# Moving an attention kernel's output projection into the gaps of late units, and its last piece into half of the last V's place

## The chip, the core and the metric

The kernel runs on one core of one Trainium2 chip. The metric is the device time of one execution in microseconds (us), as a median of several runs.

The engines of the core are named as in the profile: PE (matrix engine), DVE (vector engine), ACT (scalar engine), POOL (idle here), and SP, whose queue issues all data transfers. Each load of K, V and the weights is carried by 16 DMA engines. In lines of the profile, PEld is the weight load of PE, SPq is SP's queue, and L580 is line 580 of that kernel's file; a line number can shift by one or more between kernels.

## The reference, cut

Two layers, each a single-token decode step of attention over a long cache, followed by a small MLP block:

```python
def _A_ref(x, k_cache, v_cache, wq, wo):          # x: 2x1x576, caches: 2x32x16384x128 bf16
    q = (x @ wq) split in 32 heads of 128
    p = softmax(q . k * 128 ** -0.5)
    return (p . v, heads side by side) @ wo        # wo: 4096x576
x = x + _A_ref(_layernorm(x), ...);  x = x + _B_ref(_layernorm(x), ...)   # and once more, the same weights
```

K and V of the 2 x 32 heads are 512 MB together and are read twice, once per layer, but for two units that layer 1 still finds in place. All the rest is small.

## The kernel before

A *unit* is one head of one batch entry: 4 MB of K and 4 MB of V. A layer has 64 units. For each, half of the scores is made on PE (transposes of K chunks, then products) and half on DVE (a multiply and a sum per chunk of 1024 columns); PE weighs V one unit later.

K and V come into three *places* of 8 MB, each with a K half and a V half. The list of loads is worked off in order: a load is issued when everything that lies under its target has been used.

```python
        def kv(kind, l, i, split=False):
            ...                                   # place pl: K half at pl*place_n, V half at +unit; the last K and V in two parts
        ...
            for i in range(U):
                kv("K", l, i, split=(l == 1 and i == 2) or i == U - 1)
                ...
                    kv("V", l, i - 1)
                j, r = divmod(i - wo_at, gap)
                if r == 0 and 0 <= j < self.n_wo:
                    want_wo(l, j, wp * self.place_n + (unit if j == self.n_wo - 1 else j * self.WO_PIECE * D))
                if l == 0 and i == 6:
                    want_w2(wp * self.place_n + 5 * unit // 4)
            for i in range(U - 3, U):
                kv("V", l, i, split=i == U - 1)
            want_w34(l, 1, 1 if l == 0 else 2)     # weights of the MLP, then wq of the next layer
```

The output projection by `wo` is cut in eight pieces: seven of four heads, and one of three heads (`N_MID`). They are loaded early, into the place that the layer's last unit (63) will use: seven pieces in its K half, the last piece and `w2` in its V half. So the last K waits for the seven pieces, and the last V waits for the last piece:

```python
    def attention(self, l):
        ...
            if i == last + 1:                      # unit 57
                if l == 0:
                    self.shift_term()              # uses w2
                self.project_pieces(l, range(self.n_wo - 1))
            ...
                if i == U - 1 and c == 5:          # unit 63, after chunk 5 of 8
                    self.weigh(l, i - 2, 0)
                    self.weigh(l, i - 2, 1)
                    self.project_pieces(l, [self.n_wo - 1])
```

`project_pieces` makes the softmax normalizers on PE and DVE, scales the outputs on DVE, and runs five small matmuls per head on PE. PE's program is a hardware loop over two units at a time for units 2 to 55 of layer 0 and 12 to 55 of layer 1; its other units are straight code.

```python
        with self.nc.Block() as block:
            for e in self.ENGS:
                def run(eng, items=plan[e], loops=self.loops if e == "tensor" else ()):
```

## Time and profile before

The median was 2588.58 us in three runs. From the page of the kernel before: the busy time of each engine, the mean busy share of the 16 DMA engines in 40 slices, the bytes per second in the same slices, and the data queue with its share of 16 engines' span.

```profile
PE 1549.2 (60%) x34519; PEld 1463.6 (57%) x34519; DVE 1977.2 (76%) x2775; ACT 1112.9 (43%) x1809; POOL 0.8 (0%) x10
...
DMA  9999999999999999999899999999999999999997
GB/s 412 431 429 431 430 431 430 431 433 431 431 430 430 431 431 433 430 428 409 371 420 428 429 425 434 431 429 431 432 432 429 430 434 431 431 430 433 418 427 324
...
q1 hardware_dynamic: 51944, 1097.76, 99.1%
```

The memory stream bounds the kernel: 431 GB/s nearly everywhere, and DVE, the next, 76% busy. The dips are at the end of layer 0 (371) and at the end (324). Closer, in windows of 5 us of the kernel before (the columns are the busy time of PE, PEld, DVE, ACT and POOL with the number of instructions, the granted PE clock, the mean busy share of the DMA engines, and GB/s):

```profile
1160.00:1165.00 5.00, 3.83 (x147) 3.77 (x144) 4.90 (x7) 1.61 (x3) 0.00 (x0) 0.59 0.92 390
1165.00:1170.00 5.00, 2.20 (x20) 1.93 (x20) 4.68 (x9) 2.21 (x3) 0.00 (x0) 0.50 0.61 208
...
1265.00:1270.00 5.00, 4.96 (x148) 4.86 (x145) 4.93 (x6) 2.45 (x6) 0.00 (x0) 0.50 0.47 200
1270.00:1275.00 5.00, 1.07 (x22) 1.08 (x23) 4.21 (x10) 0.00 (x0) 0.00 (x0) 0.50 0.04 16
1275.00:1280.00 5.00, 5.00 (x160) 5.00 (x158) 3.33 (x4) 2.05 (x2) 0.00 (x0) 0.50 0.92 318
```

These are two holes: a small one at 1165 and a large one at 1270. Layer 1 has the same two near 2435 and 2540. Their causes stand in the timelines. First PE, with the start, the time, what it did, and in brackets the idle time before and what ended it:

```profile
1145.63 3.89 PE L580 MATMUL misc<-otn,buf 128*128 128x2 bf16 x140 [1.16 <-DVE otn L765]
...
1184.72 1.89 PE L670 MATMUL tps<-ident,buf 128*128 128x128 bf16 x16 [1.21 <-DMA buf<-in_A_k_cache_dram]
...
1242.98 1.89 PE L670 MATMUL tps<-ident,buf 128*128 128x128 bf16 x16 [4.58 <-DMA buf<-in_A_k_cache_dram]
```

The burst of 140 matmuls is the projection of seven pieces before unit 57; the others are the first work on K of unit 59 and of unit 62, both of which PE waited for. Then SP's queue, which shows when transfers were issued:

```profile
1141.83 0.33 SPq L359 DMA_DIRECT2D buf<-in_A_k_cache_dram  x1
...
1168.04 0.33 SPq L359 DMA_DIRECT2D buf<-in_A_k_cache_dram  x1
...
1221.82 16.81 SPq L359 DMA_DIRECT2D buf<-in_A_v_cache_dram  x2
1274.52 1.56 SPq L356 DMA_DIRECT2D buf<-in_A_v_cache_dram  x2
```

After the burst, K of unit 59 is issued 26.2 us after the K before it; elsewhere the step is 19.4 us. The last V (L356) goes out at 1274.52, some 36 us after the V before it (the second of the two in the third line). In the view of who waited for whom this is one wait of 35.9 us of SP's queue behind PE's projection (queue and line, waited for; total, times, longest):

```profile
SPq L356 <- PE misc L580: 39.2, 2, 35.9
```

And in DVE's timeline one sees why the projection of the last piece comes so late. DVE works in order, and the normalization (L765) stands behind the dot chunks, of which the last is shown:

```profile
1272.08 1.22 DVE L702 TENSOR_REDUCE sd<-prod 128x8 f32<-128x1024 bf16 x1
1273.22 0.15 DVE L750 COPY o<-ops 128x1 f32<-128x1 f32 x1
...
1273.70 0.17 DVE L765 TENSOR_TENSOR otn<-o,den 128x6 bf16<-128x6 f32 x1
```

### The profile page before, as it was taken

Reading aid. Unit: us, or ns where it says so; the run is one execution under the profiler, and the core shown is the slowest. Engines: PE = TensorE matmul, PEld = TensorE weight load, DVE = VectorE, ACT = ScalarE, POOL = GpSimd, SP = SyncE. Lnnn points to the kernel's source line nnn. Section 1 sums busy time; section 2 is a strip of 40 time slices with the busy share of each in tenths; the row PEclk is TensorE's granted clock in tenths of the full one; section 3 lists DMA queues with packets and bytes.
Section 4 is the critical chain, followed back from the end, with each engine's and each line's share of the span. In section 5 each row is a group of like instructions: output and inputs, shape, how many; then the busy total and the mean of one; then the engine's idle time right before and its main releaser. Section 6 shows DMA issues by size and latency. Waiting matters only on the chain.

```text
span 2588.1 us, 75341 instructions
## 1 busy us (share of the span) xinstructions
PE 1549.2 (60%) x34519; PEld 1463.6 (57%) x34519; DVE 1977.2 (76%) x2775; ACT 1112.9 (43%) x1809; POOL 0.8 (0%) x10
## 2 busy tenths in 40 slices
PE   5556565655565555666567765565655555655665
PEld 4555555555555555556557765555555555555655
DVE  5877787778777777878759987777777777778784
ACT  4434443444444444444335544444444444444441
POOL 0000000000000000000000000000000000000000
PEclk8666666666666666666556666666666666666665
DMA  9999999999999999999899999999999999999997
GB/s 412 431 429 431 430 431 430 431 433 431 431 430 430 431 431 433 430 428 409 371 420 428 429 425 434 431 429 431 432 432 429 430 434 431 431 430 433 418 427 324
DMA packets 52063, 1099.39 MB, mean 425 GB/s; under 512 B 4900, under 2 KB 13160, under 8 KB 16872
## 3 DMA queue, kind: packets, MB, share of 16 engines
q1 hardware_dynamic: 51944, 1097.76, 99.1%
q8 instruction: 80, 1.31, 0.2%
q14 instruction: 39, 0.32, 0.0%
HBM read 1097.74 MB, written 0.00 MB: 424 GB/s over the span
## 4 chain that ended last, share of the span: by engine, by line
DMA 52%; DVE 40%; PE 6%; SPq 1%; issue 1%; ACT 0%; DVEq 0%
DMA buf<-in_A_k_cache_dram 49%; DVE sd L702 25%; DVE prod L699 14%; PE tps L670 4%; PE misc L720 2%; DMA buf<-in_B_w_dram 2%; DVE small L722 1%; SPq L390 1%; DMA buf<-in_A_wq_dram 1%; PE misc L580 0%; SPq L373 0%; DVE small L714 0%; DVE small L712 0%; SPq L356 0%; DVE small L710 0%
## 5 line engine op out<-in xcount | busy, mean ns | idle before, releaser
L674 ACT ACTIVATE ktsb<-tps 128x1024 bf16<-128x1024 bf16 x1024 | 1006.2, 1027 | 889.2 <-PE tps L670 882.9
L702 DVE TENSOR_REDUCE sd<-prod 128x8 f32<-128x1024 bf16 x1024 | 1249.2, 1220 | 35.4
L670 PE MATMUL tps<-ident,buf 128*128 128x128 bf16 x8192 | 846.1, 271 | 647.4 <-DMA buf<-in_A_k_cache_dram 639.6
L670 PEld LDWEIGHTS tps<-ident,buf 128*128 128x128 bf16 x8192 | 686.0, 124 | 678.6 <-DMA buf<-in_A_k_cache_dram 662.5
L699 DVE TENSOR_TENSOR prod<-buf,qb 128x1024 bf16<-128x1024 bf16 x1024 | 697.7, 681 | 11.0 <-DMA buf<-in_A_k_cache_dram 10.1
L743 PE MATMUL ops<-p,buf 128*128 128x1 bf16 x16384 | 466.5, 165 | 185.8 <-DMA buf<-in_A_v_cache_dram 168.5
L743 PEld LDWEIGHTS ops<-p,buf 128*128 128x128 bf16 x16384 | 448.2, 101 | 196.1 <-DMA buf<-in_A_v_cache_dram 177.9
L687 PE MATMUL sps<-qcur,ktsb 128*128 128x1 bf16 x8192 | 352.9, 166 | 91.3 <-ACT ktsb L674 84.4
L722 DVE TENSOR_REDUCE small<-misc 128x1 f32<-128x128 f32 x128 | 37.3, 292 | 463.9 <-PE misc L720 463.9
L687 PEld LDWEIGHTS sps<-qcur,ktsb 128*128 128x128 bf16 x8192 | 319.0, 103 | 127.8 <-ACT ktsb L674 126.6
L658 ACT ACTIVATE qb<-misc 128x128 bf16<-128x128 f32 x128 | 35.5, 277 | 488.5 <-PE misc L655 488.5
L720 PE MATMUL misc<-identS,small 128*128 128x128 f32 x256 | 95.9, 478 | 51.1 <-DVE small L714 51.1
L720 PEld LDWEIGHTS misc<-identS,small 128*128 128x128 f32 x256 | 69.4, 332 | 55.8 <-DVE small L714 55.0
L731 ACT ACTIVATE p<-sd,small 128x64 bf16<-128x64 f32 x128 | 45.2, 353 | 0.0
L731 ACT ACTIVATE p<-sps,small 128x64 bf16<-128x64 f32 x128 | 40.4, 316 | 9.7 <-DVE small L722 9.7
L650 ACT ACTIVATE qcur<-qt 128x1 bf16<-128x1 bf16 x128 | 28.9, 225 | 19.4 <-DVE qt L587 19.4
L655 PE MATMUL misc<-ident,qcur 128*128 128x128 bf16 x128 | 34.1, 267 | 3.3 <-issue 2.2
L710 DVE TENSOR_REDUCE small<-sps 128x1 f32<-128x64 f32 x128 | 27.4, 214 | 0.0
L731 ACT ACTIVATION_READ_ACCUMULATOR p<-sps,small 128x1 f32 x128 | 26.9, 210 | 0.0
L712 DVE TENSOR_REDUCE small<-sd 128x1 f32<-128x64 f32 x128 | 26.6, 208 | 0.0
L731 ACT ACTIVATION_READ_ACCUMULATOR p<-sd,small 128x1 f32 x128 | 26.3, 205 | 0.0
L544 PE MATMUL sps<-xn,buf 128*128 128x2 bf16 x544 | 16.4, 166 | 14.0 <-DMA buf<-in_A_wq_dram 9.5
(75 smaller groups left out, 160.1 us busy)
## 6 DMA issues: line engine op xcount, KB each, us to landing
buf<-in_A_k_cache_dram SPq DMA_DIRECT2D x123, 4096.0 KB, 22.5
buf<-in_A_v_cache_dram SPq DMA_DIRECT2D x123, 4096.0 KB, 31.8
buf<-in_A_k_cache_dram SPq DMA_DIRECT2D x6, 2048.0 KB, 27.0
buf<-in_A_v_cache_dram SPq DMA_DIRECT2D x6, 2048.0 KB, 13.3
buf<-in_B_w_dram SPq DMA_DIRECT2D x8, 1152.0 KB, 18.4
buf<-in_A_wq_dram SPq DMA_DIRECT2D x8, 1024.0 KB, 10.2
buf<-in_A_wo_dram SPq DMA_DIRECT2D x14, 576.0 KB, 32.8
buf<-in_B_w_dram SPq DMA_DIRECT2D x2, 2160.0 KB, 27.6
```

The costliest lines, as they stand in the source:

```text
L650: self.act(lambda a: a.activation(out=self.qcur[:, q:q + 1], in_=self.qt[:, u:u + 1], func=ACT.Copy), r=["qt"], w=[f"qcur{q}"])
L655: self.pe(lambda pe: pe.matmul(self.misc[:, 0:128], lhsT=bcast(self.qcur[:, q:q + 1], 128), rhs=self.ident[:, :], start=True, stop=True), ...
L658: self.act(lambda a: a.activation(out=self.qb[q][:, :], in_=self.misc[:, 0:128], func=ACT.Copy), r=["P:misc"], w=[f"qb{q}"])
L670: ins = pe.transpose(self.tps[b][:, j * 128:(j + 1) * 128], kt[:, (j0 + j) * 128:(j0 + j + 1) * 128], self.ident[:, :])
L674: self.act(lambda a: a.activation(out=self.ktsb[k][:, :, :].rearrange("p a b -> p (a b)"), in_=self.tps[b][:, :], func=ACT.Copy), r=[f"P:t ...
L687: ins = pe.matmul(self.sps[sp][:, col:col + 1], lhsT=self.ktsb[k][:, j, :], rhs=self.qcur[:, sp:sp + 1], start=True, stop=True)
L699: self.dve(lambda v: v.tensor_tensor(out=self.prod[d][:, :, :], in0=k3, in1=bcast_mid(self.qb[q][:, :], self.CH), op=ALU.mult), r=[*res, f ...
L702: self.dve(lambda v: v.tensor_reduce(out=self.sd[q][:, o:o + self.CH], in_=self.prod[d][:, :, :], axis=AX.X, op=ALU.add), r=[f"prod{d}"], ...
L720: self.pe(lambda pe: pe.matmul(self.misc[:, 128:256], lhsT=bcast(self.m[:, q:q + 1], 128), rhs=self.identS[:, :], start=True, stop=True), ...
L722: self.dve(lambda v: v.tensor_reduce(out=self.bias[:, q:q + 1], in_=self.misc[:, 128:256], axis=AX.X, op=ALU.max, negate=True), r=["P:misc ...
L731: self.act(lambda a, c0=c0, c1=c1, src=src, part=part: a.activation(out=self.p[q][:, c0:c1], in_=src, func=ACT.Exp, bias=self.bias[:, q:q ...
L743: ins = pe.matmul(self.ops[q][:, 0:1], lhsT=vt[:, j * 128:(j + 1) * 128], rhs=self.p[q][:, h * self.TB + j:h * self.TB + j + 1], start=(h ...
```

## The change

The intent is to fill both holes. The seven pieces are projected two at a time at the ends of units 57 to 60, where PE waits for the next K. The last piece moves to the end of the V half, `w2` to its beginning, so that the first half of the last V only waits for `w2`; and the last piece is used after chunk 3 instead of 5, with its normalizers made a unit earlier.

```diff
-                    want_wo(l, j, wp * self.place_n + (unit if j == self.n_wo - 1 else j * self.WO_PIECE * D))
+                    want_wo(l, j, wp * self.place_n + (2 * unit - self.N_MID * D if j == self.n_wo - 1
+                                                            else j * self.WO_PIECE * D))
...
-                    want_w2(wp * self.place_n + 5 * unit // 4)
+                    want_w2(wp * self.place_n + unit)
...
-            if i == last + 1:
-                if l == 0:
-                    self.shift_term()
-                self.project_pieces(l, range(self.n_wo - 1))
...
-                if i == U - 1 and c == 5:
+                if i == U - 1 and c == 3:
                     self.weigh(l, i - 2, 0)
                     self.weigh(l, i - 2, 1)
+                    self.normalize(*mid, self.o[:, slice(*mid)], "o")
                     self.project_pieces(l, [self.n_wo - 1])
...
             self.row_max(l, i)
+            if i == last + 1:
+                self.normalizers(*most)
+                self.normalize(*most, self.o[:, slice(*most)], "o")
+            if last + 1 <= i <= last + 4 and pieces:
+                self.project_pieces(l, [pieces.pop(0) for _ in range(min(2, len(pieces)))])
+            if l == 0 and i == last + 4:
+                self.shift_term()
+            if i == U - 2:
+                self.normalizers(*mid)
```

(`project_pieces` no longer makes normalizers itself; `most` and `mid` are the columns of the seven pieces and of the last.)

More of the change, by code (lines that the diff above doesn't have):

```diff
@@ L784, in project, with columns @@
                  r=["P:misc", "xa"], w=["xa"])
+    def columns(self, l, js):
+        u0 = min(self.wo_piece(l, j)[0] for j in js) * self.B
+        u1 = max(self.wo_piece(l, j)[1] for j in js) * self.B
+        return u0, u1
     def project_pieces(self, l, js):
@@ L792, in project_pieces @@
         parts.sort(key=lambda p: p[0])
-        h0, h1 = parts[0][0], parts[-1][0] + parts[-1][1]
-        u0, u1 = h0 * self.B, h1 * self.B
-        self.normalizers(u0, u1)
-        self.normalize(u0, u1, self.o[:, u0:u1], "o")
-        self.project(h0, h1, parts)
+        self.project(parts[0][0], parts[-1][0] + parts[-1][1], parts)
     def attention(self, l):
@@ L805, in attention @@
         assert first < last and (last - first) % 2 == 0
+        pieces = list(range(self.n_wo - 1))
+        most, mid = self.columns(l, pieces), self.columns(l, [self.n_wo - 1])
+        assert len(pieces) <= 8
         self.s.loops.append((l * U + first, (last - first) // 2, 2))
```

## The prediction

> **What bounds the kernel.** The memory stream. The page gives the DMA queue 99.1% of the span and 1097.8 MB; the 40 slices stand near 431 GB/s (the Trainium skill, "DMA: Bandwidth & Descriptors", "Where 436 GB/s comes from", puts the fabric ceiling at 435.2; the trace agrees). DVE is 76% busy: about 16.5 us of work per unit against 19.4 us of arriving K and V. At 431 GB/s the bytes take 2547 us; the other 41 us are start, tail and holes. The holes, from windows of 5 us, as missing bytes over 431 GB/s:
> - 1160-1170: 3.1 us; 2430-2440: 2.0 us. The projection of seven pieces stands before unit 57. PE and DVE lose about 6.5 us there (PE timeline: 140 matmuls, 3.89 us, plus waits), so the next K is issued 26.2 us after the one before, not 19.4.
> - 1265-1280: 8.8 us; 2535-2550: 9.3 us. The last V cannot be issued before the last wo piece is read: the queue's waits show 35.9 and 33.6 us behind PE misc. PE is ready at 1269.5, but DVE has dot chunks (1.85 us each) in front of the normalization, so the V is issued at 1274.5.
>
> **What the change does.** No bytes change. The pieces go two at a time to the ends of units 57 to 60 (about 40 matmuls, 1.1 us), where PE idles about 4.7 us for the next K: hidden. The first hole goes.
> The first half of the last V is free after the shift term and is issued behind V62, about 1238: 4.9 us of stream moves into the hole. The last piece runs after chunk 3: two dot chunks fewer (-3.7 us). The second half is issued about 1270.9 instead of 1274.5, in old time. Old drain 1267.4 plus 4.9 is 1272.3: just in time, margin about 1 us. The second hole closes.
>
> **What comes back.** The end of attention moves only about 3.9 us earlier (2.8 us wait for V, 1.1 us at the last row maximum). In layer 0 the second w4 piece overwrites w3, which the MLP reads from about 1292.8; the queue is empty about 1295, the piece flows about 1296.3: a new hole of about 1.2 us (0 to 3). In layer 1 the weights have free places; the stream ends 9.3 us earlier, but computing (w3, GELU, w4) allows about 9.0.
> Sum: 3.1 + 8.8 - 1.2 + 2.0 + 9.0 = 21.7 us, nearly all on the critical path. I take off 1.5 us for PE's "issue" stalls (2 to 3 us each after the loops) and a slightly late second half: 20.2 us.
>
> **Prediction: 2568 us**, 8 in 10 between 2563 and 2577. Faster by over 2%: 0.005; within 2%: 0.99; slower by over 2%: 0.005.
>
> **What would show each step.** Windows: the four holes under 1 us each. The queue's timeline: one half of the last V issued with V62, the other some 32 us later. PE timeline: bursts of 40 wo matmuls ending units 57 to 60, then a wait for K of at least 2 us. A short hole before w4 in layer 0, the queue waiting for w3 matmuls. At the end, w4 matmuls hardly waiting for DMA.
>
> **What would make it wrong.** At chunk 3 V61 has not landed, or an instruction stall holds PE: 2 to 4 us of each hole stay. The hole at w4 is larger, since DVE bounds the end of attention. The slots at unit ends are too small, and K issues slip.

## The result, and the profile after

The changed kernel took 2577.97 us (2577.65 to 2578.22), against 2588.2 us before: 10.2 us or 0.4% less. The ratio is 0.996, with a 95% interval of 0.9943 to 0.9977. The two profiled executions differ by more, 12.2 us (spans 2588.1 and 2575.9), because the profiled run of the kernel before was one of its slower ones (2589.9). Both figures lie far from the 20.2 us that were predicted.

The same parts of the page after:

```profile
PE 1546.1 (60%) x34519; PEld 1459.3 (57%) x34519; DVE 1977.9 (77%) x2781; ACT 1111.2 (43%) x1809; POOL 0.8 (0%) x10
...
DMA  9999999999999999999999999999999999999998
GB/s 414 431 427 432 431 432 430 432 429 430 433 432 431 431 432 431 432 430 428 406 401 427 428 430 430 430 431 432 431 432 430 430 432 431 431 431 432 429 427 357
...
q1 hardware_dynamic: 51944, 1097.76, 99.6%
```

The same windows after, and the one where I had foretold a small new hole:

```profile
1160.00:1165.00 5.00, 0.78 (x10) 0.51 (x11) 4.56 (x11) 0.00 (x0) 0.00 (x0) 0.50 1.00 428
1165.00:1170.00 5.00, 5.00 (x81) 4.94 (x79) 1.82 (x4) 2.78 (x3) 0.00 (x0) 0.50 1.02 436
...
1265.00:1270.00 5.00, 2.46 (x92) 2.38 (x90) 4.69 (x7) 0.00 (x0) 0.00 (x0) 0.50 0.78 328
1270.00:1275.00 5.00, 5.00 (x97) 5.00 (x96) 4.44 (x7) 3.67 (x8) 0.00 (x0) 0.50 0.85 298
1275.00:1280.00 5.00, 4.05 (x135) 3.91 (x131) 3.57 (x7) 0.71 (x1) 0.00 (x0) 0.50 0.96 404
1295.00:1300.00 5.00, 2.10 (x76) 2.01 (x73) 1.26 (x4) 0.49 (x2) 0.00 (x0) 0.50 0.89 321
```

The first hole is gone entirely (208 became 436 GB/s). The second is mostly filled. SP's queue after:

```profile
1141.61 0.33 SPq L359 DMA_DIRECT2D buf<-in_A_k_cache_dram  x1
...
1162.01 0.33 SPq L359 DMA_DIRECT2D buf<-in_A_k_cache_dram  x1
...
1221.63 17.61 SPq L359 DMA_DIRECT2D buf<-in_A_v_cache_dram  x2
1239.28 31.49 SPq L356 DMA_DIRECT2D buf<-in_A_v_cache_dram  x2
```

K of unit 59 goes out 6.0 us earlier. The two halves of the last V go out at 1239.28 and 1270.45 (the 31.49 us of the merged line run to the end of the second issue, 1270.77); I had predicted 1238 and 1270.9. So the machinery does what was intended, to about a microsecond. And yet PE's timeline after says:

```profile
1164.78 1.23 PE L581 MATMUL misc<-otn,buf 128*128 128x2 bf16 x40 [4.22 <-DVE otn L766]
...
1182.71 1.23 PE L581 MATMUL misc<-otn,buf 128*128 128x2 bf16 x40 [0.37 <-ACT qb L659]
...
1184.53 1.89 PE L671 MATMUL tps<-ident,buf 128*128 128x128 bf16 x16 [0.60 <-DMA buf<-in_A_k_cache_dram]
...
1242.84 1.89 PE L671 MATMUL tps<-ident,buf 128*128 128x128 bf16 x16 [3.83 <-DMA buf<-in_A_k_cache_dram]
```

K of unit 59, issued 6.0 us earlier, comes 0.19 us earlier. K of unit 62 comes at 1242.84 instead of 1242.98. The first hole is gone from the mean rate, and nothing arrives sooner for it. That is the riddle.

**Sixteen landings, not one.** The Trainium skill says in "DMA: Bandwidth & Descriptors", section "Why a DMA increments its semaphore by 16 and not by 1", that a DMA runs on up to 16 engines that finish independently, each adding one to the semaphore, and that only the full 16 means that all data have landed. The trace has these sixteen increments with their times, though no name of an engine. Below, for some transfers, the time of the median of the sixteen landings and of the last (us from the span's start; computed from the trace's landing records):

```text
                              before            after
transfer (layer 0)         median    last    median    last
one load near 1030 us      1030.6  1038.0    1030.5  1037.8
K of unit 62               1239.5  1242.9    1236.1  1242.8
V of unit 62               1268.7  1273.0    1266.7  1272.9
last V, first half         1281.9  1282.3    1271.6  1277.8
last V, second half        1286.8  1288.1    1277.7  1282.7
wq, the last of it         1323.2  1324.8    1315.6  1319.0
```

One of the sixteen lands far behind the others: 7.4 us behind the median at 1038, and 7.3 after the change. The engine that lands second to last is there only 2.6 us behind the median. Everything that waits for a transfer waits for the last: PE begins on K of unit 62 at 1242.98, when the last landing was at 1242.93. So the lagging engine sets the pace, and the other fifteen run ahead of it with slack. The hole at 1165 was theirs: they had emptied their queues while the lagging one was still at work. For V of unit 57 and K of unit 59, on either side of the hole, the first landings are 14.8 us apart (1164.89 and 1179.68), and the last ones 9.7 us (1174.97 and 1184.68), as far apart as between any two such loads. Afterwards, in the kernel before, the lag is 4.7 us instead of 8.3: the fast engines have lost their lead, the slow one has lost nothing.

The second hole is 8.8 us long in the mean rate, but on the lagging engine only about 4.3 us: its landings of V of unit 62 and of the next half V are 9.2 us apart, and such a half takes 4.9 us. After the change they are 4.9 us apart. The lagging engine no longer waits at all there.

**Where the lag comes from.** The lag grows in steps of 1.0 us. The trace has, besides the data queue, two queues of instruction fetches: one of 16 KB packets, 80 in all, only while PE runs straight code; and one of 8 KB packets. In layer 0, the 8 KB packets of 324 to 333 ns come 119 to 125 us apart, about 121 us in the mean. In that time DVE goes through some 6 units (19.8 us each, wo included) of 21 recorded instructions, so about 128 of them per packet, as an estimate from the trace. Each packet is followed within 10 us by a step of the lag (kernel before):

```text
8 KB fetch at        290.7  412.2  532.4  657.5  778.2  898.5  1019.5  1138.3
next landing, lag     1.55   2.59   3.46   4.46   5.44   6.43    7.38    8.37
```

A second series, of 309 ns packets about 180 us apart, moves another landing by 0.7 us each time. "Runtime: NRT & Kernel Launch", section "Instruction fetch mechanics", of the Trainium skill says that instructions are streamed through a DMA queue while the program runs, and calls the cost mostly hidden. Here the transfer of data pays for it.

This gives two theories. **S**: the slowest DMA engine sets the time; a hole in the mean rate costs only what that engine idles. **M**, which my prediction used: the mean stream sets the time, and every missing byte costs.

### The profile page after: what moved, and what is told of

Read it like the earlier page. It is cut to its first block, busy times and chain, and to the rows that moved or that the text cites. A ratio compares the mean times of both kernels' runs of the same rounds, so it can differ in the third digit from the quotient of the medians.

```text
span 2575.9 us, 75345 instructions
## 1 busy us (share of the span) xinstructions
PE 1546.1 (60%) x34519; PEld 1459.3 (57%) x34519; DVE 1977.9 (77%) x2781; ACT 1111.2 (43%) x1809; POOL 0.8 (0%) x10
## 4 chain that ended last, share of the span: by engine, by line
DMA 54%; DVE 38%; PE 6%; SPq 1%; issue 1%; ACT 0%; DVEq 0%
DMA buf<-in_A_k_cache_dram 52%; DVE sd L703 24%; DVE prod L700 13%; PE tps L671 4%; DMA buf<-in_B_w_dram 2%; PE misc L721 2%; DVE small L723 1%; SPq L390 1%; DMA buf<-in_A_wq_dram 1%; SPq L373 0%; PE misc L581 0%; DVE small L715 0%; DVE small L713 0%; DVE small L711 0%; PE misc L493 0%
```

## The experiments

Eleven kernels were run, five rounds each beside the kernel before (2588.4 to 2589.2 us). All gave the right result. The change itself came first, again:

> The changed kernel itself, again, beside the others on one chip. Expected 2578 us (2577 to 2579), ratio to before 0.996, as measured before.

Measured: 2578.07 us, ratio 0.9958 (0.9945 to 0.9972).

### The spreading alone

```diff
 (the changed kernel, with)
-... (2 * unit - self.N_MID * D if j == self.n_wo - 1 ...)
+... (unit if j == self.n_wo - 1 ...)
-                    want_w2(wp * self.place_n + unit)
+                    want_w2(wp * self.place_n + 5 * unit // 4)
-                if i == U - 1 and c == 3:
+                if i == U - 1 and c == 5:
```

> The projection of seven pieces is spread over the ends of units 57 to 60, but the last piece and w2 stay in the places of the kernel before and the last piece is used after chunk 5. Theory S (the slowest of the 16 DMA engines sets the time; the fast ones run up to 8 us ahead of it, so the first hole in the mean rate is only theirs): the landing of K of unit 62 moved by 0.14 us between the two kernels, so the gain is 0 to 1 us, about 2587.5 us. Rival M (the mean stream, as I predicted: every missing byte costs): the first holes are worth 3.1 + 2.0 = 5.1 us, about 2583 us.

Measured: 2588.03 us, ratio 0.9999 (0.9985 to 1.0012). No gain clear of noise; the 5.1 us of M would be a ratio of 0.998, outside the interval. Its first windows have no hole, and K of unit 62 comes when it always came:

```profile
1160.00:1165.00 5.00, 0.77 (x3) 0.50 (x3) 4.77 (x11) 0.04 (x1) 0.00 (x0) 0.50 1.00 424
1165.00:1170.00 5.00, 5.00 (x93) 4.94 (x94) 1.61 (x4) 2.74 (x3) 0.00 (x0) 0.62 0.99 423
```

```profile
1243.04 1.89 PE L670 MATMUL tps<-ident,buf 128*128 128x128 bf16 x16 [4.15 <-DMA buf<-in_A_k_cache_dram]
```

M is refuted for the first holes: 5 us of missing bytes were brought back, and were worth nothing that can be measured.

### The place of the last piece alone

```diff
 (the changed kernel, with the seven pieces back in one burst before unit 57)
+            if i == last + 1:
+                if l == 0:
+                    self.shift_term()
+                self.normalizers(*most)
+                self.normalize(*most, self.o[:, slice(*most)], "o")
+                self.project_pieces(l, pieces)
             early = l == 1 and 1 <= i <= 4
```

> The other part alone: the last piece in the second half of the last V's place, w2 moved, piece used after chunk 3, but the seven pieces still in one burst before unit 57. Theory S: the whole gain of the change, 9 to 12 us, about 2578 us, although the first hole in the mean rate is still there. Rival M: the change less the first holes, so 5 us slower than the changed kernel, about 2583 us.

Measured: 2577.67 us, ratio 0.9958 (0.9944 to 0.9972), the whole gain, with the first hole still there (390 and 202 GB/s in the two windows). The burst of 140 matmuls, which looked like the fault of the kernel before, cost nothing that can be measured.

### The last piece later

```diff
-                if i == U - 1 and c == 3:
+                if i == U - 1 and c == 5:
```

> The changed kernel, but with the last piece used after chunk 5 instead of chunk 3, so that the second half of the last V is issued about 3.7 us later. Theory S: the slowest engine is still busy with the first half until then (its landing of the first half, 1277.8 us, less the 2.9 us from issue to first landing of new data, gives an issue deadline of about 1274.9 us; the issue comes at about 1274.5 us), so 0 to 1.5 us slower than the changed kernel, about 2579 us. Rival M: the mean stream has run dry at about 1269 us, so each of the two holes grows by 3.7 us: about 2585 us.

Measured: 2577.54 us, ratio 0.9957 (0.9943 to 0.9971). No loss. SP's queue and a window of this kernel:

```profile
1238.93 35.56 SPq L356 DMA_DIRECT2D buf<-in_A_v_cache_dram  x2
```

```profile
1270.00:1275.00 5.00, 1.43 (x29) 1.43 (x30) 4.21 (x9) 0.00 (x0) 0.00 (x0) 0.50 0.16 66
```

The second half of the last V goes out at 1274.16 instead of 1270.45, the mean rate in this window falls from 298 to 66 GB/s, and the median landing of that half moves from 1277.7 to 1281.4. The last landing stays at 1282.7 in both. So of the whole change only the place counts: that the first half of the last V need not wait. (The spreading and the earlier chunk were each taken away alone, not both together; this is read from the two runs and the one before them.)

### Taking the fetches away

In the looped units the only thing in DVE's program that changes from turn to turn is the column to which it copies the weighed V. With that copy on ACT, DVE can run in the loop that PE has.

```diff
-                def run(eng, items=plan[e], loops=self.loops if e == "tensor" else ()):
+                def run(eng, items=plan[e], loops=self.loops if e in ("tensor", "vector") else ()):
...
-            self.dve(lambda v: v.tensor_copy(out=self.o[:, u:u + 1], in_=self.ops[q][:, 0:1]),
-                     r=[f"P:ops{q}"], w=["o"])
+            self.act(lambda a: a.activation(out=self.o[:, u:u + 1], in_=self.ops[q][:, 0:1], func=ACT.Copy),
+                     r=[f"P:ops{q}"], w=["o"])
```

> The changed kernel with the same loops on DVE that PE has already (units 2 to 55 of layer 0, 12 to 55 of layer 1); to allow it, ACT instead of DVE copies the weighed V to its column. Work and bytes stay; DVE's instruction fetches in those units (one of 8 KB about every 118 us, each of which made the slowest DMA engine land 1.0 us later from then on) go. Theory S: the slowest engine's lag at the end of layer 0 falls from 8.3 us to that of the next one, about 2.6 us, and in layer 1 from 4.6 to 1.4-2.4 us: 5 to 10 us faster than the changed kernel, about 2570 us. Rival M: 0.2 MB less of 1098 MB, under 1 us: about 2578 us.

Measured: 2572.11 us, ratio 0.9935 (0.9921 to 0.9948): 6.0 us faster than the changed kernel of the call before (6.5 us when each is set against the kernel before of its own call), and, with the kernel that loops ACT too, the fastest. The queue of 8 KB fetches (packets, MB, share of 16 engines) of this kernel, after the one of the changed kernel, and its K of unit 62:

```profile
q14 instruction: 39, 0.32, 0.0%
```

```profile
q14 instruction: 25, 0.20, 0.0%
```

```profile
1238.13 1.89 PE L671 MATMUL tps<-ident,buf 128*128 128x128 bf16 x16 [4.31 <-DMA buf<-in_A_k_cache_dram]
```

Fourteen fetches fewer, 0.12 MB of 1098, and K of unit 62 comes 4.7 us earlier. The median landing of that K did not move (1235.9 against 1236.1); the last fell from 1242.8 to 1238.1. Fourteen steps of 1.0 us would have been more than 6.0; but the lag at this K only fell from 6.7 to 2.2 us, because other engines then land last. This run changes two things, the loop and the engine of the copy; in the run with ACT looped too (under "What remains") DVE makes a copy in each turn again, and the gain stays.

### Doubling the fetches, on DVE and elsewhere

```diff
 (row_max, after the last of its three DVE instructions)
+            for n in range(21):
+                v.sem_inc(self.s._sem("spare"))      # nobody waits for it
```

> The changed kernel with 21 idle semaphore increments more per unit on DVE after the row maximum, where DVE waits about 3.7 us for the next K anyway. This doubles DVE's instruction stream and so its fetches, and nothing else. Theory S: the lag of the slowest engine grows twice as fast: 8 to 16 us slower than the changed kernel, about 2590 us. Rival M: 0.17 MB more, under 1 us: about 2578.5 us.

Measured: 2604.28 us, ratio 1.0059 (1.0045 to 1.0073): 26 us slower than the changed kernel, more than the 8 to 16 that I had written. The queue of this kernel shows why the size was off:

```profile
q14 instruction: 60, 0.49, 0.0%
```

I had counted only the fetches in the looped units; there are 21 more in all, so about 1.2 us each (26.2 over 21). The 21 fetches for 21 increments in each of 128 units are again 128 instructions to a packet. Why it is 1.2 us and not 1.0 stays open. It is not that DVE had become the bottleneck by the time of these instructions: it still waits 3.9 and 4.0 us for PE and the next K, at 818 and 838 us. In layer 0 the lag reaches 11 to 12 us and then grows no further, while the mean rate falls (421, 416, 425 GB/s in later slices of the page). This fits that the fast engines then run dry.

The same instructions on POOL, behind one dummy write per unit that waits for DVE's row maximum:

```diff
+        def f(g):
+            for n in range(21):
+                g.sem_inc(self.s._sem("spare"))
+            return g.memset(self.idle[:, i:i + 1], 0.0)
+        self.pool(f, r=[f"m{q}"], w=[("idle", i)])
```

> The same 21 increments per unit, but on POOL, which is idle and follows DVE's row maximum. The same bytes of fetches, but by another engine's stream. Theory S, if POOL's instructions are fetched by another DMA engine than DVE's: a second engine lags as far as the first, the slowest does not change: 0 to 2 us slower than the changed kernel, about 2579 us. If they share one DMA engine: as the doubled DVE stream. A rival that any fetch costs the whole stream: as much as the doubled DVE stream.

Measured: 2578.74 us, ratio 0.996 (0.9947 to 0.9974), 0.7 us slower than the changed kernel of the call before (0.1 us when each is set against the kernel before of its own call), with 62 packets in the queue instead of 39. So 23 fetches more are nearly free here, while 21 more of DVE cost 26 us. At 1038 us, the second to last landing has now a lag of 4.7 us instead of 2.6, and the last one is where it was. In these two runs, fetches cost where they delay the landing that is already last, and elsewhere almost nothing.

### The same loop in the kernel before

> The kernel before, with the loops on DVE. Theory S: K lands earlier by the slowest engine's lag that goes, everything after it too, while the wait for the last V stays: about 6 us faster than the kernel before, 2582.5 us. A rival, that the hole at the last V absorbs the lag wholly in the kernel before (all engines wait there anyway): 0 to 1 us, 2588 us.

Measured: 2581.45 us, ratio 0.9973 (0.9959 to 0.9987), 7 us faster than the kernel before, with the wait for the last V still in it (9.4 us between the two last landings). The gains of the place and of the loop add up: about 10.5 us and 6 to 7 us.

### What remains

ACT in the loop too, with POOL making the small copies whose column changes:

```diff
+                def run(eng, items=plan[e], loops=self.loops if e in ("tensor", "vector", "scalar") else ()):
...
+            self.pool(lambda g: g.tensor_copy(out=self.qcur[:, q:q + 1], in_=self.qt[:, u:u + 1]), ...)
+            self.pool(lambda g: g.tensor_copy(out=self.lsum[:, u, :], in_=self.lsq[:, q, :]), ...)
+            self.pool(lambda g: g.tensor_copy(out=self.o[:, u:u + 1], in_=self.oq[:, q:q + 1]), ...)
```

> The changed kernel with the loops on DVE and on ACT as well; POOL makes the three small copies per unit whose column changes. In the run with DVE alone looped, the engine that lands last at 1131 us is 3.7 us behind the median and the next only 0.4 us; its steps of 0.7 us fall together with the fetches of the stream that remains, ACT's. Theory S: that lag goes in layer 0, in layer 1 the rest of the lag comes from PE's fetches between 1345 and 1560 us and stays: 2 to 4 us faster than with DVE alone, about 2569 us. Rival M (mean stream): no change, 2572 us or a little slower for POOL's copies.

Measured: 2572.18 us, ratio 0.9936 (0.9923 to 0.995). No gain, so the expectation of 2 to 4 us failed. The lag did go as expected in the looped part (0.5 us at 1031 instead of 2.9, the last landing 2.3 us earlier than with DVE looped alone), but the lead shrank to 1.5 us at 1149 and nothing at 1238, was 0.7 us at 1258, and nothing at 1306. From unit 56 on PE runs straight code, and its 16 KB fetches delay the landings of other engines, which then are the last (after the first, at 1125.2, the lag goes from 0.4 to 1.8 us).

PE's loop of layer 0 begun at unit 22 instead of 2:

```diff
-        first, last = (2, self.ROT)[l], U - 8
+        first, last = (22, self.ROT)[l], U - 8
```

> The changed kernel with PE's loop of layer 0 starting at unit 22 instead of unit 2, so that 20 units more are fetched as straight code: about 40 fetches of 16 KB. If PE's fetches go to the DMA engines in turn, each engine gets 2 to 3 of them at 1 us each: 2 to 4 us slower, about 2581 us. If one engine serves them all: about 40 us slower. Mean stream: 0.65 MB, 1.5 us.

Measured: 2581.15 us, ratio 0.9972 (0.9958 to 0.9985): 3.1 us slower than the changed kernel, with this many 16 KB fetches instead of 80:

```profile
q8 instruction: 120, 1.97, 0.3%
```

Forty fetches for 3.1 us fit a spread over the 16 engines (2.5 each), and not one engine that carries them all.

Last, the version with DVE looped, and in layer 1 the loops, with the change from three places to two that they need, from unit 6 on (`ROT = 12` became `ROT = 6`):

> The version with DVE looped, and in layer 1 the two-place order of K and V, and with it the loops of PE and DVE, begin at unit 6 instead of 12. About 12 fetches of 16 KB fewer for PE, spread over the engines, and one or two of 8 KB. Theory S: 3.1 us were measured for 40 such fetches more, so about 1 us faster than with DVE looped alone, 2571 us, if the two places are enough for the units that catch up after the layer's start; if they are not, DVE's rate (16.5 us per unit against 19.4) leaves the memory waiting and it is slower, by up to 10 us. Rival M: no change or slower.

Measured: 2581.09 us, ratio 0.9971 (0.9957 to 0.9985), 9 us slower. Thirteen fetches fewer (67), but in the window from 1390 to 1415 us the rate is 232 GB/s instead of 424: about 11.5 us of stream are missing, over 431 GB/s. Two places are too few for the units that catch up, the case that the expectation had named: the next K is issued at 1412.76 instead of 1396.17, since SP's queue waits for PE and then DVE to be done with the unit that lies in its place (23.0 and 9.0 us at the longest). Here a hole in the mean rate is one for the lagging engine too (its landings are 21.9 us apart, from 1404.3 to 1426.2, instead of 10.9), and it costs.

## Why the prediction was wrong

- **The bound.** "The memory stream" was right, but I read it as one stream with a mean rate. It is sixteen, and the last one counts. That is the step that failed: "The holes, from windows of 5 us, as missing bytes over 431 GB/s". The four holes went into the sum with 3.1, 8.8, 2.0 and 9.0 us; by the last landings the lagging engine idled 0, 4.3, 0 and 4.3 us in them. These 8.6 us are most of what came back.
- **"The first hole goes"**, 3.1 and 2.0 us. It went, and was worth nothing measurable: the spreading alone gave 2588.03 us against 2588.59. The hole belonged to the fast engines.
- **"The second hole closes"**, 8.8 and 9.3 (or 9.0) us. It closed as described, with issue times right to about 1 us. But on the lagging engine it was 4.3 us in each layer (9.2 us between two last landings, less 4.9 us for the half V itself; in layer 1 it was 2543.5 to 2552.7, and 2537.0 to 2541.9 after the change). These are 8.6 of the 12.2 us between the two profiled executions.
- **The rest of the gain**, some 3.6 us in the two traces. About 1.3 us in layer 0 and 1.5 in layer 1 come after the last V, between the landing of its first half and that of the last weights. In the kernel before all engines start level after the hole, so each fetch shows at once (the two halves of the last V land 5.9 us apart, not 4.9); after the change most of them hide behind the lagging engine. This is consistent with the traces, but no run tests it by itself. The remaining 0.8 us are small shifts.
- **"A new hole of about 1.2 us"** before `w4`. It is there in the mean rate (321 GB/s from 1295 to 1300, 1.3 us), and costs nothing: the last landings of the weights go on at 1295.2, 1300.5 and 1304.7 us, in steps that fit their sizes.
- **"About 40 matmuls, 1.1 us ... hidden"**. 1.23 us, and hidden. "Then a wait for K of at least 2 us" held at one of the four ends of units of layer 0 (4.00 us) and not at the others (none, 0.60 and 0.28 us).
- **"The end of attention moves only about 3.9 us earlier"**: 4.5 us (PE's first statistics of the MLP at 1286.56 instead of 1291.07).
- **"w4 matmuls hardly waiting for DMA"** at the end. Wrong; the waits went from 4.84 and 1.98 to 2.70 and 1.94 us. Computing did not take over, the lagging engine still decided. Before, and after:

```profile
2577.05 2.14 PE L580 MATMUL misc<-prod,buf 128*128 128x2 bf16 x75 [4.84 <-DMA buf<-in_B_w_dram]
2581.17 1.76 PE L580 MATMUL misc<-prod,buf 128*128 128x2 bf16 x60 [1.98 <-DMA buf<-in_B_w_dram]
```

```profile
2564.80 2.14 PE L581 MATMUL misc<-prod,buf 128*128 128x2 bf16 x75 [2.70 <-DMA buf<-in_B_w_dram]
2568.89 1.76 PE L581 MATMUL misc<-prod,buf 128*128 128x2 bf16 x60 [1.94 <-DMA buf<-in_B_w_dram]
```

- **What I listed as dangers** (V61 not landed, a stall at chunk 3, slots too small) did not matter; with the piece two chunks later the time was the same.

The trace before held the sign. I took 1267.4 us for the drain of the queue, because the mean rate fell there. But the last landing of V of unit 62 was at 1273.0, and the last two packets of it, 32 KB each, ran one after the other from 1270.2 to 1272.6: one engine was still at work (in windows of half a microsecond, two of 66 GB/s among empty ones).

What stays open: the trace does not name the DMA engines. That DVE's fetches fall on one of them and always the same is inferred from the steps of the lag, from the runs without and with twice the fetches, and from the run on POOL. Why an 8 KB fetch, 0.32 us long in the record, sets its engine back by 1.0 us is not explained.

## What to carry to other kernels

Where a kernel waits for memory, look at the last of the sixteen landings of each transfer and not at the mean rate: fill a gap only if the engine that lands last idles in it. If K or V does not arrive sooner after an edit that issues it earlier, that engine did not idle. Straight code of an engine was fetched at the cost of the same data stream; in a kernel that is bound by memory, looping an engine's program can be worth trying, here 6 us of 2578 for 14 fetches of 8 KB, beside some 10.5 us for the better order of loads. Test the parts of a change one by one: here two lines about places in the buffer carried all of it, and the spreading, which was most of the diff, carried nothing.

## What the Trainium skill lacked or had wrong

- "Runtime: NRT & Kernel Launch", section "Instruction fetch mechanics", says that crossing a block boundary costs one bump of a DMA tail and is mostly hidden, and that kernels prefer full unrolling where possible. Here 21 fetches more of DVE cost 26 us (about 1.2 us each), looping DVE won 6 us, and 40 blocks more of PE cost 3.1 us. The runs show the cost as a later last landing of the data (4.7 us at K of unit 62), and not as a wait of DVE.
- The same section gives blocks of 16 KiB for all. The trace agrees for PE (packets of 16384 B), but the packets of the other queue, whose number follows DVE's, ACT's and POOL's programs in the runs, have 8192 B.
- No page says that one engine's instruction fetches can gather on one DMA engine. That they do is inferred here: the lag of the last of 16 landings grew by 1.0 us about every 121 us, up to 8.4 us in the kernel before, and 0.5 us at most is left of it at 1031 us when DVE and ACT run in loops.
- "DMA: Bandwidth & Descriptors", section "Why a DMA increments its semaphore by 16 and not by 1", is right that the engines finish independently. It gives no size for the spread: here the last lands up to 8.4 us after the median in the kernel before, for transfers of 4 MB that take 9.7 us.
- The same page, in "Latency and other measured facts", says that engines 7 and 15 are usually slower, and ties this, as a best guess, to descriptor rings of another path. Here one engine lags without that path (all loads are issued by SP), and the lag follows the fetches; which engine it is, the trace does not tell.
